# Attention and two gated MLP stages on one core: one-column sums, a copy moved to GpSimd, Strassen sums left in PSUM, low parts in halves

## The chip, the cores and the metric

The kernel runs on one NeuronCore of a Trainium2 chip. The metric is the device time of one execution in microseconds, the median over several runs. Engines are named as in the profile: PE is TensorE (PEld its weight loads), DVE is VectorE, ACT is ScalarE, POOL is GpSimd, SP issues the transfers.

## The reference

Two batches of eight heads, 576 positions, head dimension 64, all in float32. First comes attention with a bias made by a small network from the distance of two positions; then a mixture of four experts (512 to 1024 to 512) over the 1152 tokens; then a layer 512 to 2048 to 512 whose activation is a rational function.

```python
scores = q @ k.T / 8 + bias                    # bias: relu(x*w1 + b1) @ w2, x from |i - j| and i
attn = exp(scores - max(scores))
attn = attn / (sum(attn) + 1e-09)
x = (attn @ v), tokens by 512
for e in range(4):                             # first stage
    out += p[:, e:e+1] * (relu(x @ w1[e]) @ w2[e])
h = out @ w_in                                 # second stage
g = (a0 + a1*h + a2*h**2 + a3*h**3) / (1 + |b0|*|h| + |b1|*h**2 + 1e-6)
y = g @ w_out
```

## The kernel before, in words

Every float32 product is made of products of "high" and "low" parts: the high part is the value rounded by a copy to the fp32r type (on ACT), the low part is the rest, one subtraction (on POOL for weights, on DVE where the value lies in PSUM). Three matmuls (high by high, high by low, low by high) stand for one.

**Bias phase** (`bias_phase`), then **attention** (`schedule`). Attention handles eight groups n of two heads, each in nine units g: scores into PSUM (L583), DVE adds the bias and takes the row's extreme (`biased`, L597), ACT makes the exponentials and their row sums (`exps`, L605), DVE adds 1e-9 to the sums (`norm_add`, L610, over one or two columns, with a constant tile `eps` as second operand) and takes the reciprocal (L615), POOL scales the row (`norm`, L626), PE transposes it (L643), ACT and DVE split the transposed tile into high and low (L668, L672), PE multiplies with v (L691). In the ninth unit of a group, DVE copies 64 columns of the scaled row behind it (`repeat`, L619: a maximum of a tile with itself) before the transposes. The order of these operations on each engine is worked out while the program is built, by a small planner (`Flow`): each operation has an engine, a duration, predecessors, buffers that it takes and frees, and an urgency, which is the unit's number plus an offset from the table `CFG`; the smallest urgency among those that can start goes first. The offsets of a kind are four numbers, for n = 0, n = 1, n = 2 to 6 and n = 7. Only the order goes into the program; the engines then run as their semaphores let them.

**First stage** (`first_stage`). After two pairs of hidden columns in the plain way, pairs p = 2 to 15 of 256 hidden columns use a Strassen form: seven products (`seven`) of 12 matmuls each in place of eight. Products 0, 4, 5 and 6 go into PSUM bank pair `y`, products 1, 3 and 2 into bank pair `x`; each pair exists once (`bufs=1`). Partial results are kept in SBUF by ACT (`keep`, L990); `finish` adds such a kept tile to the PSUM sum, by DVE into the SBUF tile (L994), and `relu` makes the high part on ACT (L922) and, deferred to the next `flush`, the low part on DVE (L923). After each product PE works off one tile of the down projection of the pair before (`down`, L892, six matmuls of 512 columns), whose result DVE adds up in SBUF (L898). Two more such tiles follow the seventh product. Product 0 of the next pair needs bank pair `y` again, so it waits for the low part of product 6.

Between these, `tick` takes one step of `conv_f64`, which rewrites the second stage's float64 weights as float32: per half chunk an ACT step and four DVE steps of 512 columns (L348, L350, L352, L354), SBUF to SBUF. The loop around it:

```python
for i, _ in enumerate(seven(p)):
    tick(i < 6)
    flush()
    self.down(p - 1, i)
    tick(i < 6)
```

Weights for coming pairs come by DMA; `load_parts` makes the high part on ACT (L289) and the low part on POOL (L293, one subtraction of 1024 columns), `load_differences` forms Strassen's weight differences on POOL (L320) and their high and low parts (L313, L317: three subtractions of 256, 512 and 1024 columns).

**Second stage** (`second_stage`). PE makes 128 hidden columns for 384 tokens (L1130); ACT, DVE and POOL evaluate the rational function (L1108 to L1122; POOL does one product, L1113, and the low part, L1122; DVE has three steps on SBUF operands alone, L1117 to L1119); PE multiplies with the second weights (L1138). `load_parts` also serves this stage: one weight chunk per call of `up` while chunks are queued.

## Time and profile before

| | |
|---|---|
| median of 3 runs | 830.87 us (830.5 to 833.14) |
| the profiled execution | 829.95 us, of which the span from the first to the last instruction is 828.1 us |
| busy: PE, DVE, ACT, POOL | 791.2, 696.7, 494.4, 466.2 us |
| bias phase, attention, plain start of the first stage, Strassen pairs, second stage (about) | 0 to 62, 62 to 218, 218 to 257, 257 to 600, 600 to 828 us |

In the profile a duration runs from the start of an instruction to its end, waits for a memory port included. Matmuls are pipelined, so that their durations overlap; what PE is worth in a stretch is read from the starts of like instructions.

### The profile page before, as it was taken

What the parts mean: (1) busy time and instruction counts of PE and PEld (TensorE: products, weight loads), DVE (VectorE), ACT (ScalarE), POOL (GpSimd) and SP (SyncE); (2) the same over time, 40 slices, a digit from 0 to 9 for tenths busy, and PEclk for the clock granted to TensorE, in tenths of its full rate; (3) what the DMA queues carried; (4) which work ended last, traced back from release to release, by engine and by line L of the source; (5) the groups of instructions that cost most, each with busy time, mean ns of one, the idle gap of its engine ahead of it and who ended that gap; (6) DMA issues with size and microseconds to landing.
All of it is one profiled execution on the core that took longest, in us unless ns stands there. A gap on an engine that the chain in (4) does not pass through costs nothing.

```text
span 828.1 us, 13521 instructions
## 1 busy us (share of the span) xinstructions
PE 791.2 (96%) x4980; PEld 685.6 (83%) x4980; DVE 696.7 (84%) x1160; ACT 494.4 (60%) x932; POOL 466.2 (56%) x398
## 2 busy tenths in 40 slices
PE   6988999999999999999999999999999899999997
PEld 2438888898998989998989989989788788899995
DVE  7987899999688888988788998787688878888875
ACT  6998888998434323333333334233378887878882
POOL 3287788777355345545433554542259877665552
PEclk9999999999999999999999999999999999999999
DMA  6887667551012444434434334432212211000012
GB/s 129 275 294 208 165 176 188 117 145 52 1 51 82 146 130 140 127 102 127 128 102 127 127 116 146 133 113 70 73 52 77 76 52 52 1 0 1 1 39 76
DMA packets 67633, 87.36 MB, mean 105 GB/s; under 512 B 33520, under 2 KB 42096, under 8 KB 67440
## 3 DMA queue, kind: packets, MB, share of 16 engines
q1 hardware_dynamic: 66992, 86.35, 35.3%
q8 instruction: 39, 0.64, 0.3%
q10 hardware_dynamic: 576, 0.16, 0.1%
q14 instruction: 26, 0.21, 0.1%
HBM read 60.12 MB, written 21.36 MB: 98 GB/s over the span
## 4 chain that ended last, share of the span: by engine, by line
PE 56%; DVE 18%; ACT 14%; issue 6%; POOL 4%; DMA 2%; SPq 0%; DVEq 0%; POOLq 0%; ACTq 0%
PE ps_o L892 14%; PE ps_y L984 8%; PE ps_x L984 6%; PE ps_o L1138 5%; PE ps L691 5%; PE ps_h L1130 5%; PE ps L583 4%; PE ps L643 3%; ACT hid L402 2%; ACT bo L431 2%; DVE pp L1119 2%; DVE rr L1118 2%; ACT rr L1115 2%; POOL qq L1113 2%; ACT rr L1116 2%
## 5 line engine op out<-in xcount | busy, mean ns | idle before, releaser
L892 PE MATMUL ps_o<-we,hs 128*128 128x512 f32 x810 | 203.4, 392 | 0.0
L892 PEld LDWEIGHTS ps_o<-we,hs 128*128 128x128 f32 x810 | 146.1, 188 | 25.8
L293 POOL TENSOR_TENSOR we<-wstg,we 128x1024 fp32r<-128x1024 f32 x20 | 50.3, 2517 | 131.7 <-ACT we L289 131.7
L898 DVE SCALAR_TENSOR_TENSOR acc<-ps_o,prob,acc 128x512 f32<-128x512 f32 x135 | 98.5, 743 | 24.1 <-PE ps_o L892 23.9
L1113 POOL TENSOR_TENSOR qq<-qq,ha 128x384 f32<-128x384 f32 x48 | 58.4, 1216 | 66.2 <-ACT qq L1110 66.2
L1138 PE MATMUL ps_o<-wmh,hs 128*128 128x512 f32 x252 | 85.0, 396 | 9.9 <-POOL hs L1122 5.8
L1130 PE MATMUL ps_h<-x,wmh 128*128 128x384 f32 x288 | 74.7, 340 | 0.0
L626 POOL TENSOR_SCALAR P<-P,ri 128x576 f32<-128x576 f32 x72 | 53.1, 748 | 31.7 <-DVE ri L615 19.3
L922 ACT ACTIVATE hs<-m 128x576 fp32r<-128x576 f32 x28 | 19.2, 687 | 81.2 <-DVE m L994 81.2
L1138 PEld LDWEIGHTS ps_o<-wmh,hs 128*128 128x128 f32 x252 | 47.4, 188 | 22.5 <-POOL hs L1122 7.9
L597 DVE CUSTOM_DVE_ANT_0 P<-ps,bias 128x576 f32<-128x576 f32 x72 | 53.3, 750 | 14.5 <-PE ps L583 12.2
L605 ACT ACTIVATE P<-P,nm 128x576 f32<-128x576 f32 x72 | 55.9, 777 | 5.2 <-DVE nm L597 4.9
L1117 DVE SCALAR_TENSOR_TENSOR qq<-qq,rr 128x384 f32<-128x384 f32 x48 | 33.0, 688 | 30.2 <-ACT rr L1116 28.9
L413 PE MATMUL ps_ab<-hid,wm 128*32 128x288 f32 x576 | 47.4, 427 | 10.7 <-DVE hid L405 7.3
L1122 POOL TENSOR_TENSOR hs<-pp,hs 128x384 fp32r<-128x384 f32 x48 | 52.6, 1095 | 7.2 <-issue 6.1
L317 POOL TENSOR_TENSOR wu<-wt,wu 128x1024 fp32r<-128x1024 f32 x14 | 34.6, 2468 | 38.3 <-ACT wu L313 38.3
L1130 PEld LDWEIGHTS ps_h<-x,wmh 128*128 128x128 f32 x288 | 53.5, 191 | 2.0
L984 PEld LDWEIGHTS ps_y<-x,wu 128*128 128x128 f32 x336 | 47.1, 188 | 7.2 <-DVE hs L923 5.4
L583 PE MATMUL ps<-kh,qs 128*128 128x288 f32 x168 | 51.1, 324 | 1.5 <-DVE nm L597 1.5
L984 PE MATMUL ps_y<-x,wu 128*128 128x288 f32 x336 | 49.5, 296 | 3.1 <-DVE hs L923 3.1
L405 DVE TENSOR_SCALAR hid<-ltab,shift 128x576 f32<-128x576 f32 x108 | 50.3, 545 | 0.0
L672 DVE TENSOR_TENSOR ptl<-ps,pth 128x512 fp32r<-128x512 f32 x72 | 48.4, 681 | 2.2 <-ACT pth L668 1.9
(145 smaller groups left out, 2129.9 us busy)
## 6 DMA issues: line engine op xcount, KB each, us to landing
wstg<-moe_w SPq DMA_DIRECT2D x32, 512.0 KB, 3.7
bias_d<-bo SPq DMA_DIRECT2D x9, 1152.0 KB, 5.2
bias<-bias_d SPq DMA_DIRECT2D x16, 576.0 KB, 4.9
w<-moe_w_in SPq DMA_DIRECT2D x16, 512.0 KB, 4.1
w<-moe_w_out SPq DMA_DIRECT2D x16, 512.0 KB, 3.7
kl<-kh SPq DMA_DIRECT2D x16, 288.0 KB, 4.4
w_u<-wmag SPq DMA_DIRECT2D x16, 256.0 KB, 2.3
w_d<-wmag SPq DMA_DIRECT2D x16, 256.0 KB, 2.4
```

What stands on the lines that cost most here:

```text
L293: nc.gpsimd.tensor_tensor(out=lo, in0=stg, in1=hi.bitcast(F32), op=ALU.subtract)
L583: nc.tensor.matmul(ps[:, half, dst:dst + w], lhsT=lhs, rhs=k[:, src:src + w], start=(i == 0), stop=(i == len(m) - 1))
L597: nc.vector.tensor_tensor_reduce(out=Pt[u][:, S * h:S * h + S].rearrange("p (a b) -> p a b", a=2), in0=ps[:, :, 0:288], in1=self.bias_t[n ...
L605: nc.scalar.activation(out=pt, in_=pt, func=AF.Exp, scale=-1.0, bias=stat.pop(g), accum_out=sums[n, c][:, h:h + 1])
L626: nc.gpsimd.tensor_scalar(out=pt[:, sl], in0=pt[:, sl], scalar1=ri, scalar2=1.0, op0=ALU.mult, op1=ALU.mult)
L892: nc.tensor.matmul(ps, lhsT=a, rhs=w[:, f, :], start=(f == i == 0), stop=(f == 1 and i == 2))
L898: nc.vector.scalar_tensor_tensor(out=acc[:, t], in0=ps, scalar=pr, in1=acc[:, t], op0=ALU.mult, op1=ALU.add)
L984: nc.tensor.matmul(ps[:, half, 0:288], lhsT=wu[:, w, i, k], rhs=x[v][:, k, 288 * half:288 * half + 288], start=(start and k == j == 0), st ...
L1113: nc.gpsimd.tensor_tensor(out=qq, in0=qq, in1=ha, op=ALU.mult)
L1122: nc.gpsimd.tensor_tensor(out=lo, in0=pp, in1=hi.bitcast(F32), op=ALU.subtract)
L1130: nc.tensor.matmul(ps, lhsT=w[:, k, fo:fo + P], rhs=v[:, k, :], start=(k == i == 0), stop=(k == 3 and i == 2))
L1138: nc.tensor.matmul(ps, lhsT=a[:, P * tt:P * tt + P], rhs=w[:, f % 2, :], start=(f == i == 0), stop=(f == 3 and i == 2))
```

## The change

Seven edits. (1) `norm_add` adds the constant as an immediate, one column per instruction, so two instructions in place of one for four of a group's five row tiles. (2) `repeat` goes; `norm` on POOL, in the ninth unit, first writes the scaled 64 columns behind the row and then scales the row. (3) The `CFG` table has other offsets, and the planner's entry for the ninth unit's scaling is .88 instead of .72. (4) `load_parts` makes the low part in two instructions of 512 columns. (5) In `load_differences` the low part of 1024 columns is two of 512. (6) `finish` leaves the sum in PSUM for two of its three uses (both in bank pair `x`), where `relu` reads it. (7) In the loop around `seven`, the second `tick` is left out at i = 5 and taken at i = 6.

```diff
-CFG = dict(S=(-35.26, 125.84, 11.17, 24.1), R=(28.28, -9.74, 22.13, 96.15), E=(77.47, 188.17, -1.12, 46), A=(-77.92, -53.94, -32.86, -44.11), N=(-111.57, 70.25, -249.51, -51.81), T=(34.96, 2.83, 2.3, 19.23), H=(-5.75, 1.88, -115.45, -94.07), L=(-18.35, 27.15, 27.92, 109.33), V=(-121.95, -66.29, -95.72, 89.51), G=(-73.67, -94.88, -129.15, -84.49), X=(-28.43, -204.69, -85.29, -12.23), sk=(45.12, -94.23, 14.39, 29.01), sq=(159.75, 35.05, 115.02, -160.75), sv=(-8.59, 47.12, 159.9, 80.49), qk=(-22.28, -71.03, -0.31, -20.89), qq=(-61.72, 5.89, 4.36, -0.46), kl=(0.11, 48.64, 36.96, 1.84), b=(-48.63, -151.45, 191.1, -105.74), NPB=5, EPS=0.05, w0=30, w1=56, w2=24, rk=(0.98, -24.04, 4.32, 130.75), rq=(-18.89, -50.07, -27.09, -70.45), rv=(-31.38, -71.82, 84.63, 47.31), st=301.74, F=207.64)
+CFG = dict(S=(-46.52, 288.45, 1.92, 183.94), R=(52.57, 7.45, 22.77, 52.37),
+           E=(8.78, 66.35, 136.28, 33.39), A=(54.83, -31.11, -46.06, -28.09),
+           N=(-626.58, -89.98, -9.93, 33.84), T=(113.2, 2.75, 2.45, -168.63),
+           H=(-177.56, -1.07, -82.55, 109.77), L=(-48.72, 27.9, 28.44, 96.87),
+           V=(-146.08, -263.34, -83.98, -64.74), G=(-184.15, 3.42, -48.28, -42.46),
+           X=(-29.7, 7.41, 30.23, 20.21), sk=(-43.56, -73.11, -25.75, -46.52),
+           sq=(-3.51, -291.22, 39.16, 11.06), sv=(-98.75, 28.99, 141.33, 65.56),
+           qk=(121.2, -104.52, -0.3, -80.11), qq=(10.66, -102.36, 4.34, 4.86),
+           kl=(62.79, 21.77, -33.52, -59.48), b=(68.47, -33.03, 128.78, 30.32), NPB=5, EPS=0.05, w0=58,
+           w1=24, w2=56, rk=(-100.56, 26.82, 232.95, -79.05), rq=(22.72, 25.18, 75.42, -71.95),
+           rv=(-58.45, -11.42, 57.85, -75.74), st=1417.27, F=50.61)
...
         def low():
-            nc.gpsimd.tensor_tensor(out=lo, in0=stg, in1=hi.bitcast(F32), op=ALU.subtract)
+            for k in range(0, a, a // 2):
+                sl = slice(k, k + a // 2)
+                nc.gpsimd.tensor_tensor(out=lo[:, sl], in0=stg[:, sl], in1=hi[:, sl].bitcast(F32), op=ALU.subtract)
             self.stage_w()
...
         parts = ((slice(0, 1), blocks[:, 0, 0:1]), (slice(1, 3), blocks[:, 1]), (slice(3, 7), wt))
+        halves = parts[:2] + ((slice(3, 5), wt[:, 0:2]), (slice(5, 7), wt[:, 2:4]))
...
-        for i in range(3):
+        for i in range(4):
             low(i)
...
-            sm = sums[n, c][:, 0:h + 1]
-            nc.vector.tensor_tensor(out=sm, in0=sm, in1=self.eps[:, 0:h + 1], op=ALU.add)
+            for i in range(h + 1):
+                sm = sums[n, c][:, i:i + 1]
+                nc.vector.tensor_scalar(out=sm, in0=sm, scalar1=1e-9, scalar2=None, op0=ALU.add)
...
-        def repeat(g):
-            pt = Pt[g // 9, 4]
-            nc.vector.tensor_tensor(out=pt[:, S:S + 64], in0=pt[:, 512:S], in1=pt[:, 512:S], op=ALU.max)
...
+            if c == 4:
+                nc.gpsimd.tensor_scalar(out=pt[:, S:S + 64], in0=pt[:, 512:S], scalar1=ri, scalar2=1.0, op0=ALU.mult, op1=ALU.mult)
             nc.gpsimd.tensor_scalar(out=pt[:, sl], in0=pt[:, sl], scalar1=ri, scalar2=1.0, op0=ALU.mult, op1=ALU.mult)
...
-        def finish(p, f, b, ps, m):
-            nc.vector.tensor_tensor(out=two(m), in0=ps[:, :, 0:288], in1=two(m), op=ALU.add)
-            relu(p, f, b, m, False)
+        def finish(p, f, b, ps, m, stays=True):
+
+            c = ps[:, :, 0:288] if stays else two(m)
+            nc.vector.tensor_tensor(out=c, in0=ps[:, :, 0:288], in1=two(m), op=ALU.add)
+            relu(p, f, b, c if stays else m, stays)
...
-            finish(p, 1, 1, y, m5)
+            finish(p, 1, 1, y, m5, False)
...
                 self.down(p - 1, i)
-                tick(i < 6)
+                tick(i != 5)
```

## Rows read from the trace of the kernel before

**Rows 1.** The page: busy time by engine, and engines in the chain that ended last

```profile
PE 791.2 (96%) x4980; PEld 685.6 (83%) x4980; DVE 696.7 (84%) x1160; ACT 494.4 (60%) x932; POOL 466.2 (56%) x398
...
PE 56%; DVE 18%; ACT 14%; issue 6%; POOL 4%; DMA 2%; SPq 0%; DVEq 0%; POOLq 0%; ACTq 0%
```

**Rows 2.** Windows: stretch, its length, busy us (instructions) of each engine, clock, DMA

```profile
80.00:200.00 120.00, 117.69 (x873) 105.92 (x872) 109.05 (x289) 107.87 (x259) 95.44 (x124) 1.00 0.61 151
257.00:580.00 323.00, 319.93 (x1875) 287.38 (x1874) 280.62 (x349) 116.79 (x181) 149.42 (x106) 1.00 0.40 121
625.00:650.00 25.00, 20.44 (x97) 17.38 (x96) 21.42 (x23) 20.62 (x36) 25.00 (x15) 0.98 0.30 98
```

**Rows 3.** Timeline, first stage: start, duration, instruction, idle before and releaser

```profile
257.50 1.75 PE L984 MATMUL ps_y<-x,wu 128*128 128x288 f32 x12
...
280.99 1.75 PE L984 MATMUL ps_y<-x,wu 128*128 128x288 f32 x12
...
301.68 2.39 POOL L317 TENSOR_TENSOR wu<-wt,wu 128x1024 fp32r<-128x1024 f32 x1 [2.96 <-ACT wu L313]
302.02 2.60 DVE L352 SCALAR_TENSOR_TENSOR wmag<-w,wmag 128x512 uint32<-128x512 uint32 x1
304.54 0.74 DVE L923 SCALAR_TENSOR_TENSOR hs<-ps_y,hs 128x576 fp32r<-128x576 f32 x1
305.34 1.86 PE L984 MATMUL ps_y<-x,wu 128*128 128x288 f32 x12 [0.70 <-DVE hs L923]
...
311.78 0.76 DVE L923 SCALAR_TENSOR_TENSOR hs<-m,hs 128x576 fp32r<-128x576 f32 x1 [0.16 <-ACT hs L922]
314.35 1.75 PE L984 MATMUL ps_x<-sums,wu 128*128 128x288 f32 x12
...
567.39 1.75 PE L984 MATMUL ps_y<-x,wu 128*128 128x288 f32 x12
```

**Rows 4.** Groups by line and form: low parts of sums, count, busy us, mean ns

```profile
L923 DVE SCALAR_TENSOR_TENSOR hs<-m,hs 128x576 fp32r<-128x576 f32 x28 | 21.5, 769 | 8.3 <-ACT hs L922 8.0
L923 DVE SCALAR_TENSOR_TENSOR hs<-ps_y,hs 128x576 fp32r<-128x576 f32 x17 | 12.8, 751 | 5.5 <-ACT hs L922 5.4
```

**Rows 5.** Groups by line and form: attention's small operations, and L350

```profile
L610 DVE TENSOR_TENSOR sm<-sm,eps 128x2 f32<-128x2 f32 x32 | 11.6, 361 | 1.3 <-ACT P L605 1.1
L610 DVE TENSOR_TENSOR sm<-sm,eps 128x1 f32<-128x1 f32 x8 | 4.9, 608 | 0.0
L615 DVE RECIPROCAL ri<-sm 128x2 f32<-128x2 f32 x32 | 5.1, 160 | 0.5
L619 DVE TENSOR_TENSOR P<-P 128x64 f32<-128x64 f32 x8 | 4.4, 551 | 0.1
L350 DVE TENSOR_SCALAR wmag<-wmag 128x512 uint32<-128x512 uint32 x32 | 32.5, 1014 | 0.1
L711 POOL TENSOR_SCALAR x<-xt 128x256 fp32r<-128x256 f32 x8 | 3.2, 406 | 4.4 <-DVE xt L704 4.4
```

**Rows 6.** Timeline, start of the first stage: POOL, DVE and PE

```profile
250.39 2.39 POOL L317 TENSOR_TENSOR wu<-wt,wu 128x1024 fp32r<-128x1024 f32 x1
251.48 1.91 DVE L956 TENSOR_TENSOR sums<-u,sums 128x576 fp32r<-128x576 f32 x1
256.00 0.50 PE L892 MATMUL ps_o<-wdh,hs 128*128 128x512 f32 x1 [1.57 <-DVE acc L896]
```

**Rows 7.** Groups by line and form: POOL subtractions of 512 and of 1024 columns

```profile
L317 POOL TENSOR_TENSOR wu<-wt,wu 128x1024 fp32r<-128x1024 f32 x14 | 34.6, 2468 | 38.3 <-ACT wu L313 38.3
L317 POOL TENSOR_TENSOR wu<-wstg,wu 128x512 fp32r<-128x512 f32 x14 | 19.2, 1370 | 18.3 <-ACT wu L313 18.2
```

**Rows 8.** Line L293 from 600 us on: ns least, median, most

```profile
L293 POOL TENSOR_TENSOR wml<-wstg,wmh x12: 2382/2694/2734, 599.3 to 723.2; 128x1024 fp32r<-128x1024 f32 x12
```

**Rows 9.** Timeline of POOL in the second stage

```profile
629.21 2.72 POOL L293 TENSOR_TENSOR wml<-wstg,wmh 128x1024 fp32r<-128x1024 f32 x1
...
634.48 2.73 POOL L293 TENSOR_TENSOR wml<-wstg,wmh 128x1024 fp32r<-128x1024 f32 x1
```

More of the change, by code (lines that the diff above doesn't have):

```diff
@@ L192, in setup_const @@
         nc.vector.memset(self.one_eps, 1.0 + 1e-6)
-        self.eps = c.tile([P, 2], F32, name="eps")
-        nc.vector.memset(self.eps, 1e-9)
         self.w_max = c.tile([P, 1], F32, name="w_max")
@@ L315, in low @@
         def low(i):
-            sl, x = parts[i]
+            sl, x = halves[i]
             nc.gpsimd.tensor_tensor(out=wu[:, 1, sl], in0=x, in1=wu[:, 0, sl].bitcast(F32), op=ALU.subtract)
@@ L804, in schedule @@
                         h = (g - 9 * n) % 2
-                        no = fl.op("POOL", .72, g + off("N", n), lambda g=g: norm(g), [ao])
-                        if last:
-                            no = fl.op("DVE", .13, g + off("A", n), lambda g=g: repeat(g), [no])
+                        no = fl.op("POOL", .88 if last else .72, g + off("N", n), lambda g=g: norm(g), [ao])
                         one, one2 = fl.hold("one", 4), fl.hold("one", 4)
```

## The prediction

> **What bounds the kernel now.** I read the page first: the busy line and the chain's shares of engines [rows 1]. PE is busy 96% of the span and carries 56% of the chain; DVE, with 84% and 18%, is the only other engine that matters throughout. So time can come only from places where PE stands still. The windows by stage [rows 2] say where to look. In attention (80 to 200 us) PE idles 2.31 of 120 us, while DVE is busy 109.05, ScalarE 107.87 and GpSimd 95.44: four engines near their limit. In the Strassen pairs (257 to 580) PE is busy 319.93 of 323 us. In the second stage's first part (625 to 650) GpSimd is busy all 25.00 us and PE only 20.44: here GpSimd leads.
>
> The timeline shows the Strassen stalls [rows 3]. Product 0 starts at 257.50, then at 280.99: a pair takes 23.49 us when nothing stalls. The start at 305.34 was released by the low part L923, which had ended at 305.28, because DVE had L352 before it, and that took 2.60 us: it began at 302.02 while GpSimd's subtraction of 1024 columns ran (301.68 to 304.07) and ended 0.55 us behind it. A DVE step with SBUF operands alone stands still while such a GpSimd instruction runs. The low part read from PSUM stays short: 751 ns on average [rows 4], against 2.60 us here. The same standing still is in attention's small steps [rows 5]: adding the constant takes 361 ns over two columns and 608 over one, though the reciprocal of the same columns takes 160; the copy of 64 columns takes 551.
>
> **The change part by part.** The base is the profiled execution's own 829.95 us (span 828.1 and 1.85 around it). The median of the runs, 830.87, lies 0.92 above it; I add that at the end.
>
> *The tick moved from i = 5 to i = 6.* The step that was in front of product 6's low part (L352 at 302.02) now comes behind it and behind the down tile's addition. At 302.02 DVE would take L923 (0.74 us) at once, or as soon as ScalarE's high part is done, and PE wants bank pair y at 281.0 + 23.5 = 304.5: L923 may begin 1.7 us later than 302.02 and is still in time. The moved step issues all that it issued: 12 ticks a pair as before; in one pair of five it carries the end of a chunk with its two transfers on SP, now a down tile later, and the store it makes is not read before the second stage. The whole stall: 567.39 − 257.50 = 309.89 us for 13 pairs [rows 3]; 13 times 23.49 is 305.37; the difference is 4.52 us. That is one end, nothing is the other. I take −4.2, because all that stood in front of L923 in the shown stall has moved. What is late next is the tick in front of L923 for product 2, whose bank is next wanted by product 1 of the following pair.
>
> *Sums in PSUM.* Bank pair x is now released by the low part and not by the addition. In the pair shown the low part of product 1 begins at 311.78 and ends at 312.54; product 3, which takes the bank next, starts at 314.35 [rows 3]. That is 1.8 us of cover, the two PE steps between. The low part costs the same from either memory (769 against 751 ns, [rows 4]). No row shows DVE writing PSUM; a longer addition costs nothing up to the 1.8 us and would cost 14 times the excess beyond; it could also be shorter, with no PE time to win. Behind the addition on DVE wait one tick and the low part, nothing of PE's sooner than product 3. I take 0. Product 2's sum has even longer until the next use of its bank.
>
> *Halves of low parts, Strassen and its start.* GpSimd's 2.4 us become two of about 1.37 [rows 7], so a DVE step waits for one half at most. In the pairs, PE is already freed by the tick; I count nothing more. Where PE stood at the start of the stage for 1.57 us (256.00), DVE's additions were late behind L956, 1.91 us long beside a 1024-column subtraction begun at 250.39 [rows 6]. It would get in at the half, near 251.7, about 1 us earlier, of which GpSimd's second half takes some back. Ends −1.57 and +0.3; I take −0.8.
>
> *Halves in the second stage.* Two of 512 cost 2 × 1370 − 2468 = 272 ns more than one of 1024 [rows 7]. While GpSimd is full, that is on the path. From one L293 to the next is 5.27 us there (629.21 to 634.48, [rows 9]), so five lie in the full 25 us: +1.3 us. Behind them on GpSimd are L1122 and L1113, for whom PE and ScalarE wait. Above: all twelve count [rows 8], +3.3. Below: DVE gets in between halves and the 0.31 us by which the median L293 exceeds its least goes, five times: −1.6. I take +1.3.
>
> *Attention, DVE.* What goes: 11.6 and 4.9 us (L610) and 4.4 (L619), 20.9 us in all [rows 5]. What comes: 8 groups × 9 columns = 72 immediates of one column. No row has such an instruction. Below, it can be taken at nothing; above, at the 608 ns of the one-column add of now, 43.8 us in all, if it waits for GpSimd as that does. L350, also a tensor_scalar, averages 1014 ns on 512 columns, so it waits; the reciprocal, a tiny step with one SBUF input, never does. I take the reciprocal's 160 ns, the nearest in size and inputs: 11.5 us, so DVE is relieved of 9.4.
>
> The Trainium skill, "SBUF — State Buffer", section Who interferes with whom, says that DVE contends with GpSimd in a two-port mode or with two SBUF inputs; "Advanced Engine Details and Errata", section VectorE Performance Modes, gives the two-port mode only to dimensions even or odd above one. By that the one-column immediate never waits and two columns at once could; [rows 5] bear out the first clause for the adds and for L350, and no run here shows the one-column immediate.
>
> *Attention, GpSimd and the path.* Eight copies of 64 columns: above 406 ns each (the 256-column one, [rows 5]), below nothing; 0.2 us, 1.6 in all, within GpSimd's 24.6 idle us of 120. They stand in front of the ninth unit's scaling, for which PE's transposes wait; a DVE step of 551 ns behind it goes. The chain is shorter by some 0.35 us and a hand-over, per group.
>
> *Attention, the new order.* Which of two ready operations goes first changes on all engines and SP's queue. For n = 2 to 6 PE's and DVE's offsets keep their sequence (T and R hardly move); ScalarE's exponentials fall behind all else (E −1.12 to 136.28), GpSimd's scaling loses its lead over the splits of k. No row shows that order; from the windows I can only bound the sum of both. The gain's upper end is DVE's 9.4 us, as if DVE were the bound throughout. PE's idle time, 2.31 × 156/120 = 3.0 us over attention's 156, is the smaller measure. The other end is a loss of 4 us, ScalarE's 12.13 idle us of 120 used up by a third in waiting. I take −4.0, near PE's row.
>
> *The constant's memset* (one instruction in the bias phase, off PE's path): 0.
>
> Sum: 829.95 − 4.2 + 0 − 0.8 + 1.3 − 4.0 = 822.25, and with 0.92 for the runs' median 823.2 us.
>
> **The rivals.** First, *attention gives nothing*: PE and ScalarE hold it, or the new order takes what DVE frees. For it: PE busy 117.69 of 120. Against: DVE in attention stands 10.95 us idle of 120 only. 826.25 + 0.92 = 827.2. Second, *the order costs 4 us* by later exponentials: for it, ScalarE is 90% busy; against, exponentials run units ahead of the transposes. 831.2. Third, slower: *the one-column adds wait for GpSimd*, in attention, at 608 ns each: 43.8 − 20.9 = 22.9 us more DVE work; DVE has 10.95 × 1.3 = 14.2 idle us there, so attention grows by 8.7: 829.95 + 8.7 − 5.0 + 1.3 + 0.92 = 835.9. It decides from (20.9 + 14.2)/72 = 0.49 us an add. For it: today's adds and L350; against: the reciprocal. Fourth, *GpSimd's halves all count* in the second stage: 829.95 − 9.0 + 3.3 + 0.92 = 825.2; for it the full 25 us, against, GpSimd has room outside them.
>
> **How the numbers follow.** The forecast has 0.55 and its own range is 816 to 827; attention nothing 0.15; order costs 0.12; adds wait 0.10; all halves 0.08. Best ends of every term: 829.95 − 4.52 − 1.57 − 1.6 − 9.4 + 0.92 = 813.8. So the range is 814 to 832, which leaves out the third rival and little else. 0.3% is about 2.5 us, what a measurement of this kernel tells from no change: faster means below 828.4. Faster: forecast, fourth and most of the first, 0.74; same: the second and the rest of the first, 0.15; slower: 0.11.
>
> **What would show it.** Right: product 0 starting every 23.5 us with no wait on L923; tensor_scalar sm rows near 0.16 us with little spread; DVE's busy share in attention lower by some 6 points; no DVE step above about 2 us beside GpSimd in the pairs; L293 rows near 1.4 us, and GpSimd still full near 625 to 650. Wrong: product 3 waiting for the low part of product 1, one-column adds of 0.5 us or more, transposes waiting for exponentials with attention as long as before.

## The result and the profile after

The kernel after takes 823.9 us (median of 4 runs, 823.53 to 824.63) where the kernel before took 831.38 us on the same chip (4 runs, 830.5 to 833.14): ratio 0.9908, 95% interval 0.989 to 0.9927. The prediction was 823.2 us. The profiled execution of after took 823.53 us, of which the span is 821.7 us.

The line numbers of after are larger by some ten: the added constant is L622, the reciprocal L627, the copy of 64 columns L635, the low part of sums L931, `finish` L1004, Strassen's products L992, its low parts of weights L328, `load_parts` L303, the second stage's products L1140 and L1148, its steps on POOL L1123 and L1132.

First the page of after, its busy line and the chain's shares by engine. They answer to [rows 1].

```profile
PE 788.9 (96%) x4980; PEld 684.5 (83%) x4980; DVE 672.2 (82%) x1183; ACT 491.5 (60%) x932; POOL 477.5 (58%) x454
...
PE 57%; ACT 18%; DVE 12%; POOL 6%; issue 4%; DMA 2%; SPq 0%; POOLq 0%; DVEq 0%; ACTq 0%
```

DVE has lost 24.5 us of busy time, and ScalarE has taken its place as the second engine of the chain. POOL is 11.3 us busier. The same stretches as in [rows 2]:

```profile
80.00:200.00 120.00, 118.72 (x889) 107.54 (x888) 101.20 (x315) 107.73 (x265) 98.92 (x133) 1.00 0.59 150
257.00:580.00 323.00, 323.00 (x1901) 291.85 (x1900) 269.94 (x351) 116.67 (x182) 153.42 (x132) 1.00 0.38 120
625.00:650.00 25.00, 20.90 (x90) 18.19 (x89) 21.44 (x25) 19.26 (x37) 23.57 (x18) 0.86 0.30 103
```

In the Strassen pairs PE has no idle time left. In attention DVE is busy 101.20 of 120 us instead of 109.05, 6.5 points of its share, and PE gets through 889 matmuls where it got through 873. In the second stage PE is no better off, and its clock is lower on the average.

The best account of the time is the length of each part, worked out from the starts of six instructions in the two traces:

| from the start of ... to the start of ... | before, us | after, us | change |
|---|---|---|---|
| the execution, to the last bias matmul | 60.15 | 60.76 | +0.61 |
| there, to the first plain product into bank pair `x` (attention) | 160.95 | 157.07 | −3.88 |
| there, to the first product 0 (start of the stage) | 36.40 | 35.45 | −0.95 |
| there, to the last product 0 (13 pairs) | 309.89 | 305.33 | −4.56 |
| there, to the first matmul of the second stage | 35.57 | 35.62 | +0.05 |
| there, to the last matmul (second stage) | 220.31 | 222.62 | +2.31 |

Three parts are shorter, the second stage and the bias phase are longer; together −6.42, which is all of the span's 6.4 us. The medians lie 7.48 us apart, because the profiled execution of before ran 1.43 us under its median and that of after 0.37.

### The profile page after: what moved, and what is told of

Its sections match the earlier page's. It is cut to its first block, busy times and chain, and to the rows that moved or that the text cites. A ratio compares the mean times of both kernels' runs of the same rounds, so it can differ in the third digit from the quotient of the medians.

```text
span 821.7 us, 13650 instructions
## 1 busy us (share of the span) xinstructions
PE 788.9 (96%) x4980; PEld 684.5 (83%) x4980; DVE 672.2 (82%) x1183; ACT 491.5 (60%) x932; POOL 477.5 (58%) x454
## 4 chain that ended last, share of the span: by engine, by line
PE 57%; ACT 18%; DVE 12%; POOL 6%; issue 4%; DMA 2%; SPq 0%; POOLq 0%; DVEq 0%; ACTq 0%
PE ps_o L900 20%; PE ps_y L992 10%; PE ps_x L992 8%; PE ps L701 6%; PE ps L594 5%; PE ps L653 4%; ACT rr L1125 3%; POOL qq L1123 3%; DVE pp L1129 3%; ACT rr L1126 3%; DVE rr L1128 3%; DVE qq L1127 3%; ACT bo L442 2%; ACT hid L413 2%; ACT hs L1131 2%
## 5 line engine op out<-in xcount | busy, mean ns | idle before, releaser
L303 POOL TENSOR_TENSOR we<-wstg,we 128x512 fp32r<-128x512 f32 x40 | 57.3, 1454 | 130.4 <-ACT we L297 130.4
L1123 POOL TENSOR_TENSOR qq<-qq,ha 128x384 f32<-128x384 f32 x48 | 58.2, 1212 | 65.8 <-ACT qq L1120 65.8
L1148 PE MATMUL ps_o<-wmh,hs 128*128 128x512 f32 x252 | 85.6, 398 | 11.0 <-POOL hs L1132 5.9
L1140 PE MATMUL ps_h<-x,wmh 128*128 128x384 f32 x288 | 75.0, 341 | 0.0
L930 ACT ACTIVATE hs<-ps_x 128x576 fp32r<-128x576 f32 x32 | 20.8, 651 | 80.6 <-DVE ps_x L1004 73.9
L1148 PEld LDWEIGHTS ps_o<-wmh,hs 128*128 128x128 f32 x252 | 47.8, 190 | 24.0 <-POOL hs L1132 8.4
L1127 DVE SCALAR_TENSOR_TENSOR qq<-qq,rr 128x384 f32<-128x384 f32 x48 | 34.8, 724 | 30.0 <-ACT rr L1126 27.8
L328 POOL TENSOR_TENSOR wu<-wt,wu 128x512 fp32r<-128x512 f32 x28 | 36.2, 1314 | 36.4 <-ACT wu L324 36.4
L1132 POOL TENSOR_TENSOR hs<-pp,hs 128x384 fp32r<-128x384 f32 x48 | 52.5, 1093 | 8.3 <-issue 6.2
L1140 PEld LDWEIGHTS ps_h<-x,wmh 128*128 128x128 f32 x288 | 53.7, 192 | 1.9
L1148 PE MATMUL ps_o<-wml,hs 128*128 128x512 f32 x126 | 49.7, 395 | 0.0
L992 PEld LDWEIGHTS ps_y<-x,wu 128*128 128x128 f32 x336 | 47.5, 188 | 2.2
```

What stands on the lines that cost most here:

```text
L303: nc.gpsimd.tensor_tensor(out=lo[:, sl], in0=stg[:, sl], in1=hi[:, sl].bitcast(F32), op=ALU.subtract)
L992: nc.tensor.matmul(ps[:, half, 0:288], lhsT=wu[:, w, i, k], rhs=x[v][:, k, 288 * half:288 * half + 288], start=(start and k == j == 0), st ...
L1123: nc.gpsimd.tensor_tensor(out=qq, in0=qq, in1=ha, op=ALU.mult)
L1127: nc.vector.scalar_tensor_tensor(out=qq, in0=qq, scalar=1.0 + 1e-6, in1=rr, op0=ALU.add, op1=ALU.mult)
L1140: nc.tensor.matmul(ps, lhsT=w[:, k, fo:fo + P], rhs=v[:, k, :], start=(k == i == 0), stop=(k == 3 and i == 2))
L1148: nc.tensor.matmul(ps, lhsT=a[:, P * tt:P * tt + P], rhs=w[:, f % 2, :], start=(f == i == 0), stop=(f == 3 and i == 2))
```

## Experiments

Twelve kernels were run besides before and after. Each was timed in turn with the kernel before on its own chip, and the ratio is to that. The lengths are those of the table above, each from one profiled execution, so a difference of a few tenths between two kernels is not read. In attention the margin is wider: before, tick_only, diff_halves_only, psum_only and parts_halves_only have the same attention, and take 160.85 to 162.28 us for it; after, whole_second and spread, which also share theirs, take 157.02 to 157.07. The clock of attention is the mean granted clock from 8 us before the last bias matmul to 12 us behind it.

| kernel | us | ratio, 95% interval | attention (clock) | start | pairs | second stage |
|---|---|---|---|---|---|---|
| before | 831.38 | | 160.95 (0.91) | 36.40 | 309.89 | 220.31 |
| after | 823.9 | 0.9908, 0.989 to 0.9927 | 157.07 (1.00) | 35.45 | 305.33 | 222.62 |
| tick_only | 827.6 | 0.9959, 0.9944 to 0.9973 | 161.51 (0.91) | 37.10 | 306.46 | 220.32 |
| diff_halves_only | 824.97 | 0.9925, 0.9902 to 0.9948 | 160.85 (1.00) | 35.17 | 305.33 | 220.29 |
| psum_only | 830.63 | 0.9999, 0.9986 to 1.0013 | 162.05 (0.91) | 36.40 | 309.34 | 220.28 |
| parts_halves_only | 834.93 | 1.0046, 1.0029 to 1.0063 | 162.28 (0.91) | 36.66 | 309.99 | 221.92 |
| add_only | 830.6 | 0.9985, 0.9973 to 0.9997 | 161.08 (0.91) | 36.78 | 309.52 | 220.26 |
| attn_ops_old_order | 831.25 | 0.9998, 0.9988 to 1.0008 | 160.96 (1.00) | 37.30 | 310.58 | 220.29 |
| order_only | 838.36 | 1.0082, 1.0067 to 1.0097 | 167.21 (1.00) | 36.54 | 309.45 | 220.35 |
| two_columns | 826.13 | 0.9935, 0.992 to 0.9949 | 159.05 (0.91) | 35.45 | 305.32 | 223.40 |
| old_add | 825.35 | 0.9913, 0.9895 to 0.9931 | 159.46 (0.91) | 35.45 | 305.33 | 221.95 |
| whole_second | 822.59 | 0.9896, 0.9881 to 0.991 | 157.02 (1.00) | 35.44 | 305.32 | 221.00 |
| spread | 826.24 | 0.994, 0.9927 to 0.9954 | 157.04 (1.00) | 35.44 | 305.31 | 224.32 |
| spread_halves | 819.85 | 0.9848, 0.9827 to 0.9868 | 158.15 (0.91) | 35.45 | 305.32 | 217.93 |

### The pairs: the tick, the halves, the sums in PSUM

**tick_only**: the kernel before with edit 7 alone.

```diff
                 self.down(p - 1, i)
-                tick(i < 6)
+                tick(i != 5)
```

> The kernel before with edit 7 alone (the second tick taken at i = 6 in place of i = 5). Theory of the prediction: the moved conversion step alone frees bank pair y in time, so the first products of the pairs start every 23.49 us with no wait on the low part, 4.5 us less from the first pair to the last, and nothing else moves: about 826.9 us where the kernel before has 831.4. Rival: the stall is gone only because GpSimd's long subtraction was cut (edit 5); then some starts still wait for the low part and at most 1 us is won, 830.4 us or more.

827.6 us, ratio 0.9959. Every period from product 0 to product 0 is 23.49 us but the first, 24.62, in which the granted clock was 0.5 (1.2 GHz) for 3.41 us; so the pairs gain 3.4 us in this execution and would have gained 4.5 without that stretch. The timeline of this kernel, at the place of [rows 3] where the stall was:

```profile
304.30 2.41 POOL L317 TENSOR_TENSOR wu<-wt,wu 128x1024 fp32r<-128x1024 f32 x1 [2.96 <-ACT wu L313]
304.79 0.76 DVE L923 SCALAR_TENSOR_TENSOR hs<-ps_y,hs 128x576 fp32r<-128x576 f32 x1
```

POOL's subtraction of 1024 columns still runs, but what DVE has to do beside it now is the low part read from PSUM, and that takes 0.76 us.

**diff_halves_only**: the kernel before with edit 5 alone, the tick where it was.

```diff
+        halves = parts[:2] + ((slice(3, 5), wt[:, 0:2]), (slice(5, 7), wt[:, 2:4]))
...
-        for i in range(3):
+        for i in range(4):
             low(i)
```

> The kernel before with edit 5 alone (the 1024-column low part of the weight differences in two halves). Theory of the prediction: it wins the 0.8 us at the start of the stage (PE's 1.57 us wait for the down tile's addition shrinks) and little in the pairs, since the step stays in front of the low part: 829.5 to 831 us. Rival: the cut is enough by itself, because a step of 2.60 us becomes one of 1.4 us and the stall of 0.6 to 0.9 us a time goes: the pairs too start every 23.49 us, 4.5 us less there, 826 us in all, and the edits 5 and 7 win the same time twice.

824.97 us, ratio 0.9925. All 13 periods are 23.49 us here too, and the start of the stage is 1.23 us shorter. The timeline of this kernel at the stall's place:

```profile
301.60 3.00 POOL L318 TENSOR_TENSOR wu<-wt,wu 128x512 fp32r<-128x512 f32 x2 [2.96 <-ACT wu L314]
301.95 1.50 DVE L353 SCALAR_TENSOR_TENSOR wmag<-w,wmag 128x512 uint32<-128x512 uint32 x1
303.37 0.74 DVE L924 SCALAR_TENSOR_TENSOR hs<-ps_y,hs 128x576 fp32r<-128x576 f32 x1
...
304.40 1.75 PE L985 MATMUL ps_y<-x,wu 128*128 128x288 f32 x12
```

The step of `conv_f64` that took 2.60 us at this place [rows 3] takes 1.50: it gets in after the first half. The low part ends at 304.11, and product 0 starts on time at 304.40. The two halves take 3.00 us together where they take 2.54 us in after (the row at 297.54 below), so the wait was shared out, not done away with. Each of the two edits removes the five stalls alone; together they remove them once.

**psum_only**: the kernel before with edit 6 alone.

```diff
...
-            nc.vector.tensor_tensor(out=two(m), in0=ps[:, :, 0:288], in1=two(m), op=ALU.add)
...
+            c = ps[:, :, 0:288] if stays else two(m)
+            nc.vector.tensor_tensor(out=c, in0=ps[:, :, 0:288], in1=two(m), op=ALU.add)
...
```

> The kernel before with edit 6 alone (two of Strassen's sums stay in PSUM). Theory of the prediction: nothing, 831.4 us within 0.5 us: product 3 does not wait for the low part of product 1 (it comes 1.8 us sooner), the five stalls of product 0 stay. Rival: ScalarE and DVE read the sums from PSUM sooner, so the low part of product 6 is earlier too and 1 us or more of the stalls goes (830 us); other rival: product 3 waits, the period is longer than 23.49 us in all pairs, 833 us or more.

830.63 us, ratio 0.9999. The long periods stay (24.30, 24.01, 24.31, 24.00 and 24.30 us). The edit is worth nothing and costs nothing.

### The second stage: low parts whole, in halves, spread

**parts_halves_only**: the kernel before with edit 4 alone.

```diff
-            nc.gpsimd.tensor_tensor(out=lo, in0=stg, in1=hi.bitcast(F32), op=ALU.subtract)
+            for k in range(0, a, a // 2):
+                sl = slice(k, k + a // 2)
+                nc.gpsimd.tensor_tensor(out=lo[:, sl], in0=stg[:, sl], in1=hi[:, sl].bitcast(F32), op=ALU.subtract)
```

> The kernel before with edit 4 alone (all weight chunks' low parts in two instructions of 512 columns). Theory: the second stage pays for it: GpSimd is full for 25 us there and each cut costs it 0.14 to 0.27 us more, and PE's longer wait brings another stretch at the lower clock: 1.0 to 2.2 us more than before between the last pair and the end; in the pairs and in attention nothing: 832.4 to 833.6 us. Rival: the loss seen there comes from the other phase at which the second stage begins and not from the cut: 831.4 us, with the second stage as long as before.

834.93 us, ratio 1.0046: slower. The second stage is 1.6 us longer. Followed from product to product against before, it is 0.7 us behind at 650 us (by before's times) and 1.5 us behind from 722 us on; old_add, which has the same halves, is 0.7 and 1.5 us behind at the same products. The ratio stands for 3.8 us, more than the 1.0 to 2.2 expected. The profiled execution is also 1.1 us longer in the bias phase, which the edit does not touch, and 1.3 us in attention; what the rest is stays open.

**whole_second**: the kernel after, low parts whole again in the second stage.

```diff
-            for k in range(0, a, a // 2):
-                sl = slice(k, k + a // 2)
+            step = a // 2 if len(key) == 2 else a
+            for k in range(0, a, step):
+                sl = slice(k, k + step)
```

> The changed kernel with edit 4 kept for the first stage's chunks only; the second stage's chunks have their low part in one instruction of 1024 columns again. Theory: the second stage's 2.2 us come back: 821.7 us where the changed kernel has 823.9; GpSimd's spacing from chunk to chunk is 5.27 us again, the stretch at the lower clock 3.41 us again. Rival: the loss came with the phase of the stage's start; then 823.9 us as with halves.

822.59 us, ratio 0.9896, whose interval overlaps that of after. By the traces the second stage is 1.6 us shorter than in after, as much as parts_halves_only lost. PE's two long waits are as before the change; the last two lines are PE's waits from 622 to 735 us (engine, tile and line, what it waited for: us in total, times, longest):

```profile
637.70 0.51 PE L1149 MATMUL ps_o<-wmh,hs 128*128 128x512 f32 x1 [1.55 <-ACT hs L1132]
640.64 0.80 PE L1149 MATMUL ps_o<-wmh,hs 128*128 128x512 f32 x1 [2.21 <-POOL hs L1133]
...
PE ps_o L1149 <- POOL hs L1133: 5.2, 4, 2.2
PE ps_o L1149 <- ACT hs L1132: 2.8, 2, 1.6
```

**spread**: whole_second, but a weight chunk only in every second call of `up`.

```diff
...
-            if loads:
+            if loads and len(F) % 2:
                 loads.pop(0)()
```

> As the one with whole low parts in the second stage, and there a weight chunk is taken only in every second call of up. Theory: GpSimd leads from 616 to 641 us because each call adds one chunk (2.4 us) to L1123 and L1132 (2.2 us unhindered), 5.3 us for 4.2 us of PE's work; with a chunk in every second call it needs 3.4 us a call unhindered, PE leads, the waits of 2.36 and 1.74 us and the stretch at the lower clock go: 4 to 6 us less than with the chunks in every call, 816 to 818 us. Rival: PE waits for ScalarE's and DVE's chain and not for GpSimd, or a chunk comes late for the block that needs it: less than 1 us.

826.24 us, ratio 0.994: worse than whole_second, where 4 to 6 us less were expected. POOL now has idle time (19.74 us busy from 625 to 650 us), and PE waits all the same. Rows of POOL and PE in this kernel, then PE's waits from 622 to 735 us:

```profile
635.45 2.38 POOL L304 TENSOR_TENSOR wml<-wstg,wmh 128x1024 fp32r<-128x1024 f32 x1
637.78 1.32 POOL L1133 TENSOR_TENSOR hs<-pp,hs 128x384 fp32r<-128x384 f32 x1
...
639.15 0.50 PE L1149 MATMUL ps_o<-wmh,hs 128*128 128x512 f32 x1 [2.29 <-POOL hs L1133]
...
678.18 0.69 PE L1149 MATMUL ps_o<-wmh,hs 128*128 128x512 f32 x1 [2.28 <-POOL hs L1133]
...
PE ps_o L1149 <- POOL hs L1133: 10.4, 5, 2.6
```

So POOL's total is not what PE waits for: a single piece of 2.38 us stands in front of the low part of `hs`, for which PE waits 2.29. The two waits near 640 us have even become one, and by before's times this kernel is 3.0 us ahead of before at 655 us. But a chunk now comes about every 9.8 us up to 723 us, and PE's wait comes back with every second one: at 690 us this kernel is 3.4 us behind, after the wait at 678.18 and 3.41 us at a granted clock of 0.5 right behind it.

**spread_halves**: whole_second, but each chunk's two halves stand behind two successive calls of `up`.

```diff
...
+            part(0)
+            if self.spread:
+                self.rest = lambda: part(step)
...
-            if loads:
+            if self.rest:
+                self.rest()
+                self.rest = None
+            elif loads:
                 loads.pop(0)()
```

> The kernel after, but in the second stage each weight chunk's low part is two halves of 512 columns, behind two successive calls that make 128 hidden columns; a chunk begins in every second call. GpSimd's own work in a call is about 1.0 + 1.2 us, with a half 3.6 us, under the 4.17 us that a call takes where nothing waits. Theory (PE waits where GpSimd's steps for the rational function stand behind a subtraction of 2.4 us and then hang in the chain of ScalarE, DVE and GpSimd): PE's two waits of 1.55 and 2.21 us near 640 us shrink under 1 us together, the stretch at the lower clock goes with them, and the second stage is 3 us or more shorter than with whole low parts in every call: 817 to 820 us. Rival (the chain through ScalarE's high part of 1024 columns and its stores is what PE waits for, whatever GpSimd's pieces): PE waits 2 us or more as with whole low parts in every second call, 824 to 827 us.

819.85 us, ratio 0.9848: the best of all, 4 us below after, and the intervals of the two ratios don't touch. The timeline of this kernel, POOL and PE, and below it PE's waits for POOL from 622 to 735 us:

```profile
635.52 1.30 POOL L307 TENSOR_TENSOR wml<-wstg,wmh 128x512 fp32r<-128x512 f32 x1
...
636.77 1.00 POOL L1142 TENSOR_TENSOR hs<-pp,hs 128x384 fp32r<-128x384 f32 x1
...
637.83 0.50 PE L1158 MATMUL ps_o<-wmh,hs 128*128 128x512 f32 x1 [1.06 <-POOL hs L1142]
...
639.62 1.62 POOL L307 TENSOR_TENSOR wml<-wstg,wmh 128x512 fp32r<-128x512 f32 x1
...
PE ps_o L1158 <- POOL hs L1142: 6.6, 6, 1.5
```

No piece of POOL's work is longer than 1.62 us here, the low part of `hs` takes 1.00 us instead of 1.33, and of PE's two waits near 640 us one is left, 1.06 us, a little more than the 1 us expected. It comes back too, up to 1.5 us long; the waits for POOL sum to 6.6 us, where spread has 10.4 and whole_second 5.2 and another 2.8 for ScalarE. Whole_second also has a wait of 0.81 us at 619.64 and 3.41 us at a granted clock of 0.5 from 640.11, and this kernel has neither. Its window, beside that of after above, shows 23.94 us of PE busy in place of 20.90, at full clock:

```profile
625.00:650.00 25.00, 23.94 (x121) 21.53 (x120) 19.43 (x28) 20.94 (x40) 20.46 (x17) 1.00 0.17 53
```

### Attention: the operations and the order

**add_only**: the kernel before with edit 1 alone; the order stays as it was.

```diff
-            sm = sums[n, c][:, 0:h + 1]
-            nc.vector.tensor_tensor(out=sm, in0=sm, in1=self.eps[:, 0:h + 1], op=ALU.add)
+            for i in range(h + 1):
+                sm = sums[n, c][:, i:i + 1]
+                nc.vector.tensor_scalar(out=sm, in0=sm, scalar1=1e-9, scalar2=None, op0=ALU.add)
```

> The kernel before with edit 1 alone: the constant as an immediate, a column at a time; every other instruction and the order on every engine as before. DVE is relieved of 16.5 us of additions and takes 72 x 0.144 = 10.4 us in their place, 6.1 us less. Theory (the relief turns into time only where the order of the work lets PE use it): attention within 1 us of before, 830.0 to 832.0 us in all. Rival (the additions were on the path by themselves, and in the run with both operations the re-planned order hid it): attention 2 to 4 us shorter, 827 to 829 us.

830.6 us, ratio 0.9985. The additions have become as short as in after (144 ns each), but attention takes 161.08 us, as before. The ratio's interval ends just below 1; what it allows is a gain of 0.2 to 2.2 us. The trace shows where one could lie. The last product with v in before (first line) and in this kernel, then this kernel's first plain product into bank pair `x`:

```profile
219.56 0.30 PE L691 MATMUL ps<-pel,splv 64*128 64x320 f32 x1
...
219.83 0.30 PE L690 MATMUL ps<-pel,splv 64*128 64x320 f32 x1
...
222.52 0.68 PE L881 MATMUL ps_x<-x,we 128*128 128x288 f32 x3 [0.99 <-DVE hs L727]
```

From the last bias matmul (60.15 and 61.44 us) to the last product with v it is 159.41 us in before and 158.39 here, 1.0 us less; the other kernels with before's attention have 159.31 to 160.74. Then PE waits 0.99 us for DVE, a wait that before has not, and the gain is gone. One execution shows this; what the edit is worth by itself, about 1 us, is not proved by it.

**attn_ops_old_order**: the kernel before with edits 1 and 2 and the planner's entry of .88, and the old table of offsets.

```diff
...
-                        no = fl.op("POOL", .72, g + off("N", n), lambda g=g: norm(g), [ao])
-                        if last:
-                            no = fl.op("DVE", .13, g + off("A", n), lambda g=g: repeat(g), [no])
+                        no = fl.op("POOL", .88 if last else .72, g + off("N", n), lambda g=g: norm(g), [ao])
```

> The kernel before with edits 1 and 2 alone (constant by the column, 64 columns copied on GpSimd; the planner's entry for the ninth scaling .88), with the old table of offsets. Theory of the prediction: the relief of DVE is the cause of attention's 3.3 us; so most of it comes here, 2.5 to 3.5 us less up to the last product with v: 828 to 829 us. Rival: the old order was laid out for the old operations and keeps PE's sequence as it was, and the gain is the new order's: 0 to 1 us less, 830.5 to 831.5 us.

831.25 us, ratio 0.9998; attention 160.96 us: nothing won, as the rival had it. The planner works the order out anew, so the old offsets with the new operations are not exactly the old order.

**order_only**: the kernel before with the new offsets and nothing else.

```diff
-CFG = dict(S=(-35.26, 125.84, 11.17, 24.1), ...
+CFG = dict(S=(-46.52, 288.45, 1.92, 183.94), ...
```

> The kernel before with the new table of offsets alone (edit 3 without the .88). Theory of the prediction: order alone gives little, 0 to 1 us either way: 830.5 to 832.5 us. Rival: the order is the cause: 2.5 us or more less with the old operations too, 829 us or less. If both this and the run with the operations alone give little, the two need each other.

838.36 us, ratio 1.0082; attention 6.3 us longer, a loss that neither theory nor rival had. PE's waits from 62 to 222 us in this kernel begin with this line (as above: us in total, times, longest):

```profile
PE ps L593 <- DVE nm L607: 3.6, 8, 0.7
```

In before the same wait for DVE's extremes is 1.5 us, in after 1.3; but in diff_halves_only, whose attention is that of before, it is 2.8, so this wait accounts for 0.8 to 2.1 us of the loss. All of PE's idle time up to the last product with v is 9.71 us here and 5.80 in before. So the new offsets are a loss without the operations, and the operations are worth nothing without the offsets; together they are worth 3.9 us. Which operation the offsets need, old_add below tells.

**two_columns**: the kernel after, the immediate added to both columns at once.

```diff
-            for i in range(h + 1):
-                sm = sums[n, c][:, i:i + 1]
-                nc.vector.tensor_scalar(out=sm, in0=sm, scalar1=1e-9, scalar2=None, op0=ALU.add)
+            sm = sums[n, c][:, 0:h + 1]
+            nc.vector.tensor_scalar(out=sm, in0=sm, scalar1=1e-9, scalar2=None, op0=ALU.add)
```

> The changed kernel, with the constant added over two columns in one immediate instruction instead of one column each. Theory (a row's form decides, one column never stands beside GpSimd's instruction, two do): the two-column additions range from 0.15 to above 1 us like the old ones, 0.36 us on average, attention loses 0.5 to 1.5 us: 824.5 to 825.5 us. Rival: an immediate with one SBUF operand of any such small width never waits; then 32 instructions fewer on DVE (4.6 us of its time) and 0 to 0.5 us less than the changed kernel: 823.4 to 823.9 us.

826.13 us, ratio 0.9935. The groups of this addition in two_columns, by form:

```profile
L621 DVE TENSOR_SCALAR sm<-sm 128x2 f32<-128x2 f32 x32 | 14.8, 463 | 1.9 <-ACT P L616 1.7
...
L621 DVE TENSOR_SCALAR sm<-sm 128x1 f32<-128x1 f32 x8 | 1.1, 140 | 0.0
```

The ratio's interval overlaps that of after; the traces tell more. One column takes 140 ns and two take 463, the longest 1375, so the rival, by which they never wait, fell. Attention is 0.9 us longer than in spread_halves and 2.0 longer than in after. Only the first is a fair comparison: attention of two_columns and of spread_halves began with 3.41 us at a granted clock of 0.5, that of after did not.

**old_add**: the kernel after with the addition of before, a tensor and a constant tile.

```diff
-            for i in range(h + 1):
-                sm = sums[n, c][:, i:i + 1]
-                nc.vector.tensor_scalar(out=sm, in0=sm, scalar1=1e-9, scalar2=None, op0=ALU.add)
+            sm = sums[n, c][:, 0:h + 1]
+            nc.vector.tensor_tensor(out=sm, in0=sm, in1=self.eps[:, 0:h + 1], op=ALU.add)
```

> The kernel after with the addition of before (a tensor and a constant tile, both columns at once); the order on every engine is that of after but for the 72 columns added singly. Theory (at the new order what DVE loses in an addition beside GpSimd is on the path): the additions take 0.35 us or more each again, 5 to 6 us in all, and attention is 1.5 to 3 us longer than in the kernel after: 825.5 to 827 us. Rival (with two columns at once, what cost 2.2 us was a stretch at the lower clock, not the additions): as the kernel after, 823.5 to 824.5 us, with rows at the same 0.35 us.

825.35 us, ratio 0.9913, whose interval overlaps that of after: the times do not separate the two. The groups of the addition in old_add:

```profile
L623 DVE TENSOR_TENSOR sm<-sm,eps 128x2 f32<-128x2 f32 x32 | 14.4, 450 | 1.9 <-ACT P L618 1.7
L623 DVE TENSOR_TENSOR sm<-sm,eps 128x1 f32<-128x1 f32 x8 | 3.4, 423 | 0.0
```

By the traces attention is 1.3 us longer than in spread_halves, which has the same operations otherwise and the same clock. PE's order is the same in all of these kernels, so they can be followed from matmul to matmul against after. spread_halves falls 1.1 us behind in the first 6 us, where its stretch at the lower clock lies, and stays there; whole_second and spread, without the stretch, keep within 0.06 us. two_columns and old_add are 1.2 and 0.9 us behind 60 us after the last bias matmul, and 2.0 and 2.4 in the end. So both accounts hold a part: some 1 us is the stretch, and 0.8 us in two_columns and 1.5 in old_add came where the clock was full and only the additions differ, each in one execution.

old_add also tells what the new offsets need. It has them with the old additions and with edit 2, and its attention, 159.46 us, is 1.5 us or more below that of the four kernels that have before's attention and the lower clock (160.95 to 162.28); order_only, without edit 2, has 167.21. It is edit 2, the copy on GpSimd with its entry in the planner (by which the order comes out otherwise too), that turns the offsets from a loss into a gain.

## Why the prediction held, step by step

**The tick** (taken at −4.2, at most −4.52): the pairs gained 4.56 us and PE's periods are 23.49 us throughout. The rows of after that answer to [rows 3], three starts of product 0 and the seam of two pairs:

```profile
253.28 0.95 PE L992 MATMUL ps_y<-x,wu 128*128 128x288 f32 x6
...
276.77 0.42 PE L992 MATMUL ps_y<-x,wu 128*128 128x288 f32 x2
...
297.54 2.54 POOL L328 TENSOR_TENSOR wu<-wt,wu 128x512 fp32r<-128x512 f32 x2 [2.94 <-ACT wu L324]
298.03 0.76 DVE L931 SCALAR_TENSOR_TENSOR hs<-ps_y,hs 128x576 fp32r<-128x576 f32 x1
298.71 0.74 DVE L906 SCALAR_TENSOR_TENSOR acc<-ps_o,prob,acc 128x512 f32<-128x512 f32 x1
299.37 1.27 DVE L363 SCALAR_TENSOR_TENSOR wmag<-w,wmag 128x512 uint32<-128x512 uint32 x1
300.26 1.75 PE L992 MATMUL ps_y<-x,wu 128*128 128x288 f32 x12
...
558.61 0.56 PE L992 MATMUL ps_y<-x,wu 128*128 128x288 f32 x3
```

The low part L931 now stands in front of the moved step L363 and has 1.5 us to spare before 300.26. The value was right. For the halves of edit 5 the prediction counted nothing in the pairs, since PE is "already freed by the tick". That is right, but it did not say that the halves would have freed PE by themselves. tick_only and diff_halves_only show that the 4.5 us belong to either.

**Sums in PSUM** (0): right. The sums and low parts of after by form, which answer to [rows 4]:

```profile
L931 DVE SCALAR_TENSOR_TENSOR hs<-ps_x,hs 128x576 fp32r<-128x576 f32 x32 | 24.2, 757 | 10.8 <-ACT hs L930 9.1
...
L931 DVE SCALAR_TENSOR_TENSOR hs<-m,hs 128x576 fp32r<-128x576 f32 x14 | 11.5, 821 | 3.0 <-ACT hs L930 3.0
L1004 DVE TENSOR_TENSOR ps_x<-ps_x,m 128x576 f32<-128x576 f32 x14 | 10.7, 766 | 6.4 <-PE ps_x L992 6.4
L1004 DVE TENSOR_TENSOR m<-ps_y,m 128x576 f32<-128x576 f32 x14 | 10.6, 755 | 2.3 <-PE ps_y L992 2.1
```

The addition that no row of before showed, DVE into PSUM, takes 766 ns against 755 into SBUF; the later release of the bank stays inside the 1.8 us of cover, and product 3 waited in no pair.

**The start of the stage** (−0.8): −0.95. At the place of [rows 6] the timeline of after has

```profile
247.40 3.06 POOL L328 TENSOR_TENSOR wu<-wt,wu 128x512 fp32r<-128x512 f32 x2
248.48 0.82 DVE L964 TENSOR_TENSOR sums<-u,sums 128x576 fp32r<-128x576 f32 x1
249.34 1.73 DVE L958 TENSOR_TENSOR u<-u,m 128x576 f32<-128x576 f32 x1
251.79 0.50 PE L900 MATMUL ps_o<-wdh,hs 128*128 128x512 f32 x1 [0.61 <-DVE acc L904]
```

DVE's addition L964 gets in between the halves (0.82 us, where its counterpart took 1.91), the next one still waits for the second half, and PE's wait of 1.57 us is 0.61. diff_halves_only has this gain (1.23 us) and tick_only does not, so the cause is the halves, as the prediction had it.

**Halves in the second stage** (+1.3): the two kernels that tell the edit by itself, parts_halves_only and old_add, are 1.5 us behind in the end; the sign and nearly the size were right, but the size by luck, since two errors cancelled. The full POOL's spacing from chunk to chunk grew by 0.14 us and not by 0.27, from 5.27 us [rows 9] to 5.40, because a pair of halves takes 2.86 us there where a whole took 2.72. Five of these give the 0.7 us by 650 us; as much again came with the next chunks, up to 722 us, outside the stretch to which the prediction confined it. POOL's rows in after, then PE's two waits:

```profile
620.60 2.86 POOL L303 TENSOR_TENSOR wml<-wstg,wmh 128x512 fp32r<-128x512 f32 x2
...
625.99 2.87 POOL L303 TENSOR_TENSOR wml<-wstg,wmh 128x512 fp32r<-128x512 f32 x2
...
637.88 0.50 PE L1148 MATMUL ps_o<-wmh,hs 128*128 128x512 f32 x1 [1.74 <-ACT hs L1131]
...
640.95 0.80 PE L1148 MATMUL ps_o<-wmh,hs 128*128 128x512 f32 x1 [2.36 <-POOL hs L1132]
```

After lost 2.3 us in this stage. The 0.7 or 0.8 us beyond the halves' 1.5 came between 678 and 704 us, where PE waits for `hs` from ScalarE and POOL; whole_second has it too (221.00 us against 220.31), old_add, whose second stage is the same, has not. What brings it stays open.

**Attention** (−4.0): −3.9 between the two traces. At like clocks it is −3.8 at the full one (diff_halves_only's 160.85 to 157.07) and −2.8 to −4.1 with the stretch at the lower one (160.95 to 162.28 in four kernels, 158.15 in spread_halves). The small operations of after, answering to [rows 5]:

```profile
L622 DVE TENSOR_SCALAR sm<-sm 128x1 f32<-128x1 f32 x72 | 8.3, 146 | 1.8 <-ACT P L616 1.4
...
L627 DVE RECIPROCAL ri<-sm 128x2 f32<-128x2 f32 x32 | 5.2, 162 | 0.6
L635 POOL TENSOR_SCALAR P<-P,ri 128x64 f32<-128x64 f32 x8 | 2.5, 318 | 1.4 <-ACT xt L708 0.9 <-DVE ri L627 0.4
```

The one-column immediate takes 146 ns on the mean, 134 at least and 155 at most: the reciprocal's 160 ns were the right neighbour (the 72 keep DVE busy for 8.3 us, overlaps counted once, where 11.5 were taken), and the rival by which it waits for POOL fell. The copy on GpSimd takes 318 ns where 200 were taken. The Trainium skill, "SBUF — State Buffer", section Who interferes with whom, lets DVE contend with GpSimd only with two SBUF inputs or in a two-port mode, and "Advanced Engine Details and Errata", section VectorE Performance Modes, gives that mode to even dimensions and to odd ones above one; the one column at 134 to 155 ns and the two columns at 463 agree with both. The value was right, its reason was not: −4.0 was a choice between a gain of 9.4 us and a loss of 4, and that it fell so near is luck. DVE's relief alone gave nothing to the whole (add_only, attn_ops_old_order), which is what the first rival said of it, and the new offsets by themselves cost 6.3 us, more than the second rival's 4. The prediction let PE's sequence stand for n = 2 to 6; in the trace of after only the first 214 of some 730 groups of like matmuls are in before's sequence. Its measure, PE's idle time, was too small at 3.0 us: from the last bias matmul to the last product with v PE idles 5.80 us in before (5.80 to 7.07 with the other kernels of that attention) and 4.33 in after. That is 1.5 of the 3.9 us between the two (2.6 of 3.8 against diff_halves_only, both at the full clock); where the rest was won the waits do not show, and it stays open.

**The memset**: 0 taken. The bias phase is 0.61 us longer in after and 0.2 to 1.3 us longer in the other profiled kernels, some of which, as diff_halves_only with 1.26, did not touch the constant; nothing is read from it.

**The sum**: 822.25 us for a profiled execution, and it took 823.53. The parts that were counted came out otherwise by −0.36 (tick), −0.15 (start), +1.01 (second stage) and +0.12 us (attention); the bias phase, taken at 0, adds 0.61. The 0.92 us that were added for the median were 0.37 in after, so that the forecast of 823.2 and the measured 823.9 lie closer together than the two sums do is in part luck.

## What to carry to other kernels

When two edits remove the same stall, each looks decisive and the sum counts it once: run each alone before crediting either. A shared port or a full engine is relieved less by fewer microseconds than by shorter pieces in the right places: in the second stage two halves of a GpSimd instruction back to back cost 1.5 us against the whole one, and the same halves behind two different calls gained 3.1 us against it (221.00 to 217.93), where whole ones in every second call lost 3.3 (224.32). Offsets of a planner and the operations that it orders are one edit; here the operations under the old offsets won nothing, and the offsets under the old operations cost 6.3 us of attention.

## What was not expected of the hardware

A DVE addition of one column with an immediate never waited for GpSimd: of the 72 in after, 46 began while a GpSimd instruction ran, and all took 134 to 155 ns. The same addition over two columns took 463 ns on the mean and up to 1375 (580 for the 23 of 32 that began beside GpSimd, 164 for the others). Two single columns at 146 ns are 0.29 us, less than one instruction for both.

A longer stretch at the lower clock need not cost. In after the granted clock fell to 0.5 (1.2 GHz) for 6.83 us at 639.9 us, in before for 3.41 us at 649.0. The windows of after around it, before and from the fall on:

```profile
632.00:641.00 9.00, 4.90 (x23) 3.48 (x21) 7.60 (x9) 8.09 (x15) 9.00 (x8) 0.94 0.22 66
641.00:652.00 11.00, 11.00 (x42) 10.05 (x43) 9.50 (x13) 7.90 (x16) 8.36 (x7) 0.74 0.25 89
```

PE had been busy 4.90 of 9 us. add_only and order_only have the longer stretch with whole low parts: they are 1.05 us behind before right after it, 0.25 us from 668 us on (by before's times), and within 0.1 us from 704 us on. Before waits at these two places, 0.53 us for POOL at 668.01 and 0.92 for ScalarE at 702.11, and in the two kernels the first wait is gone and the second is 0.71 and 0.73. At attention's start 3.41 us of it cost 1.1 us with the new operations and order (158.15 against 157.02 to 157.07, one execution); with the old ones attention took 160.95 to 162.28 us with it and 160.85 without.
